# Second layer's weight conversion in five steps that pause while output tiles wait, its low bits from VectorE, and zero rows of q and k by DMA

## The chip, the cores and the metric

One core of one Trainium2 chip runs the whole program. The metric is the time of one execution on the device in microseconds (us), given as the median of several runs. The core's engines are TensorE (PE; its weight loads are listed as PEld), VectorE (DVE), ScalarE (ACT), GpSimd (POOL) and SyncE (SP). Each works through its own queue in order. SP and POOL issue the DMA transfers, which share 16 DMA engines.

## The reference

A gated linear attention over a sequence (768 steps, 4 batches, 8 heads of 48), then two feed-forward layers on its 3072 rows of 384 values, the second with a normalisation first:

```python
for t in range(S):
    state = alpha[:, :, t, :, None] * state + einsum('bhd,bhe->bhde', k[:, :, t], v[:, :, t])
    y[:, :, t] = einsum('bhd,bhde->bhe', q[:, :, t], state)
x = y.transpose(0, 2, 1, 3).reshape(B * S, H * D)
# layer 1
g = x @ w_gate; val = x @ w_val
x = (g / (1 + exp(-g))) * val @ w_out
# layer 2: the same after
xn = x / sqrt(mean(x * x) + 1e-6) * rms_g
```

The weights of the layers arrive as 64-bit floating-point numbers (`w1`, `w2` are handed over as pairs of 32-bit integers: a high word and a low word). The kernel has to make 32-bit numbers of them itself.

## The kernel before

**Blocks and pieces.** The 3072 rows are 24 chunks of 128 rows. Three chunks make a block of 384 rows, so each layer has eight blocks, named (0, 0) to (0, 7) for layer 1 and (1, 0) to (1, 7) for layer 2. A block runs over 12 slices f of the 1536 hidden values. For each slice `mlp_points` makes `g` (gate) and `v` (value) with 9 matmuls each (three terms of a high and low split of weights and inputs), and 9 matmuls of `o` (output) of the slice before. I call these 27 matmuls a period. ACT computes `s` from `g` (L593) and the rounded copy `hh` (L602); DVE multiplies `s` by `v` (L596) and makes the remainder `hl` (L608). There is one buffer of `g`, one of `v` and one set of three `o` tiles.

**The end of a block.** The three `o` tiles of a finished block wait in a list, `self.later`. `evac` takes one tile per point of the program: ACT copies it out to `ev` (L549; two buffers, each free again when its store has landed) and, in layer 1, squares it back into `o` (L552). Only then may TensorE write the next block's first piece into this tile, which happens at the end of the next block's second period.

**The conversion.** `conv(layer)` is a generator that turns the 12 raw weight slices into 32-bit ones: ACT takes the absolute value of the high word (L150, `room<-wraw`) and spreads the top three bits of the low word (L155, `wraw<-wraw`); DVE clamps (L156), shifts and joins the low bits (L158) and joins the sign (L163). For layer 2, whose input is split at once, ACT also makes the high part of the slice before (L178) and DVE its low part (L182). For layer 2 it goes through four steps for each slice, and `run` calls it three times per period with a rate (`CONV2` = 0.75 steps each time) during the blocks (0, 7) and (1, 0). The raw words come by SP's queue, three transfers a slice, two slices ahead. `norm_steps` (transposes `xt` on PE, `xhi` on ACT, `xlo` on DVE) prepares the inputs of layer 2 in the same blocks.

**What sets the order.** Every engine gets its instructions in the order in which this Python program emits them. A step of `conv` that is emitted between two uses of an engine stands between them in its queue.

**The start.** The tiles `qk` hold q, k and alpha of a chunk in 48 of each 64 partitions; the 16 others must be zero. POOL clears both whole tiles with memsets (L653, L654); the loads of `qk` (L93, SP's queue) follow these, since they write into the same tiles. POOL then issues the raw words of layer 1.

Of the kernel before, what the change touches and what calls it, by code (L numbers as in the profile page):

```python
# [13 lines left out]
AF = mybir.ActivationFunctionType  # L14
ALU = mybir.AluOpType
# [4 lines left out]
B, H, S, D = 4, 8, 768, 48  # L20
NT, DM, DFF = B * S, H * D, 1536
C = 128
NCB = S // C
NCH = B * NCB
NP = H // 2
# [10 lines left out]
PRE = 0.2  # L36
CONV1, CONV2 = 1.34, 0.75
EXTRA = 4
# [16 lines left out]
class Kernel:  # L55


    def __init__(self, tc, ctx, qka, vl, vlx, vn, qn, dirx, w1, w2, g2, mask, ident, out):
        self.tc, self.nc, self.ctx = tc, tc.nc, ctx
# [21 lines left out]
        self.ssq = const.tile([128, NCH], F32, name="ssq")  # L81
        self.mask_d, self.ident_d, self.g2_d = mask, ident, g2
        self.W, self.X, self.P = {}, {}, {}
# [49 lines left out]
    def conv(self, layer):  # L133
# [8 lines left out]
        nc = self.nc  # L142
        ahead = 2 if layer else 3
        R = {f: self.raw(layer, f) for f in range(ahead)}
        yield
        for f in range(NF):
            xf = self.xtile(layer, f)
            xi = xf.bitcast(I32)
            hi, lo = R[f][:, :, 1], R[f][:, :, 0]
            nc.scalar.activation(out=xf, in_=hi.bitcast(F32), func=AF.Abs, scale=65536.0)  # L150
            if layer and f:
                self.split_hi(layer, f - 1)
            yield
            top = R[f].rearrange("p f t -> p (f t)").bitcast(mybir.dt.uint8).rearrange("p (f b) -> p f b", b=8)[:, :, 3]
            nc.scalar.activation(out=lo, in_=top, func=AF.Copy, scale=1 / 32, bias=-15.5 / 32)  # L155
            nc.vector.tensor_scalar(out=xf, in0=xf, scalar1=W_MIN, scalar2=W_MAX, op0=ALU.max, op1=ALU.min)  # L156
            yield
            nc.vector.scalar_tensor_tensor(out=xi, in0=xi, scalar=3, in1=lo,  # L158
                                           op0=ALU.logical_shift_left, op1=ALU.bitwise_or)
            if layer and f:  # L160
                self.split_lo(layer, f - 1)
                yield
# [486 lines left out]
    def run(self):  # L649
        nc = self.nc  # L650
        nb = len(BLOCKS[0])
        self.where = {FIRST[0][j] + i: (j, i) for j, m in enumerate(BLOCKS[0]) for i in range(m)}
        nc.gpsimd.memset(self.qk[0], 0.0)  # L653
        nc.gpsimd.memset(self.qk[1], 0.0)  # L654
        nc.gpsimd.memset(self.pt32, 0.0)
# [39 lines left out]
        for gj, f, piece in self.mlp_points():  # L695
# [31 lines left out]
            if gj in ((0, 0), (0, 1)) and self.split_ok(gj, f):  # L727
                next(self.sp, None)
            if gj in ((0, nb - 1), (1, 0)) and self.ready[1] < self.freed + EXTRA - 1:
                conv(1, CONV2)  # L730
# [10 lines left out]
def _layout(inputs):  # L741
# [26 lines left out]
    for pre in ("moe_", "moe2_"):  # L768
# [8 lines left out]
    return dict(qka=qka, vl=vl, vlx=vlx, vn=vn, qn=qn, dirx=dirx, w1=ws[0], w2=ws[1], g2=g2, mask=mask,  # L777
                ident=np.eye(128, dtype=np.float32))

# [11 lines left out]
```

## Time and profile before

| | |
|---|---|
| time, median of 3 runs | 1154.93 us (1153.11 to 1155.69) |
| profiled execution | 1155.11 us; its span in the trace 1153.3 us |
| PE busy | 1096.6 us (95% of the span) |
| PEld busy | 1028.5 us (89%) |
| DVE busy | 635.0 us (55%) |
| ACT busy | 452.1 us (39%) |
| POOL busy | 47.3 us (4%) |
| chain that ended last | PE 83%, ACT 3%, DVE 2% |

Busy time is a sum over the whole program. The times of single instructions are given from the start of the span. A timeline row has start, duration, engine, line and operation; in square brackets stands how long the engine had been idle before it and which instruction ended that. The granted TensorE clock is a share of full speed: 1.00 and 0.50 are its two levels, 2.4 and 1.2 GHz. About a tenth of the program is the attention's start, some 120 us in which PE has gaps; from there to the end PE is nearly always busy, apart from the blocks (0, 7) and (1, 0), from 620 to 745 us.

### The profile page before, as it was taken

Reading aid. Unit: us, or ns where it says so; the run is one execution under the profiler, and the core shown is the slowest. Engines: PE = TensorE matmul, PEld = TensorE weight load, DVE = VectorE, ACT = ScalarE, POOL = GpSimd, SP = SyncE. Lnnn points to the kernel's source line nnn. Section 1 sums busy time; section 2 is a strip of 40 time slices with the busy share of each in tenths; the row PEclk is TensorE's granted clock in tenths of the full one; section 3 lists DMA queues with packets and bytes.
Section 4 is the critical chain, followed back from the end, with each engine's and each line's share of the span. In section 5 each row is a group of like instructions: output and inputs, shape, how many; then the busy total and the mean of one; then the engine's idle time right before and its main releaser. Section 6 shows DMA issues by size and latency. Waiting matters only on the chain.

```text
span 1153.3 us, 31352 instructions
## 1 busy us (share of the span) xinstructions
PE 1096.6 (95%) x13812; PEld 1028.5 (89%) x13812; DVE 635.0 (55%) x1336; ACT 452.1 (39%) x884; POOL 47.3 (4%) x79
## 2 busy tenths in 40 slices
PE   2579999999999999999999999999999999999998
PEld 2455569999999999999999989999999999999998
DVE  4779867876776767677663767622222223222221
ACT  3365625543343443433445555422222223222222
POOL 2112000000000000000000000000000000000000
PEclk9779999999999999999999998999999999999999
DMA  8767544444544443544423444010101010101000
GB/s 259 207 190 253 155 105 140 110 124 122 132 138 109 133 128 103 139 128 125 142 78 127 145 159 143 4 41 1 41 1 42 2 41 2 41 1 42 1 21 21
DMA packets 58936, 112.26 MB, mean 97 GB/s; under 512 B 7664, under 2 KB 47856, under 8 KB 58800
## 3 DMA queue, kind: packets, MB, share of 16 engines
q1 hardware_dynamic: 53616, 89.02, 27.0%
q0 software_dynamic: 5184, 21.24, 5.4%
q8 instruction: 108, 1.77, 0.7%
q14 instruction: 28, 0.23, 0.1%
HBM read 97.26 MB, written 12.98 MB: 96 GB/s over the span
## 4 chain that ended last, share of the span: by engine, by line
PE 83%; ACT 3%; DVE 2%; issue 1%; DMA 1%; ACTq 0%; DVEq 0%
PE g L587 25%; PE o L628 25%; PE v L587 24%; PE y L320 3%; PE sb L268 2%; PE y L309 1%; PE sa L268 1%; PE kv L333 1%; PE xt L537 1%; PE kp L432 1%; PE y L305 1%; DMA out<-ev 1%; ACT ev L549 0%; ACT room L150 0%; DVE s L596 0%
## 5 line engine op out<-in xcount | busy, mean ns | idle before, releaser
L596 DVE TENSOR_TENSOR s<-s,v 128x384 f32<-128x384 f32 x192 | 106.3, 554 | 390.8 <-PE v L587 363.5
L587 PE MATMUL g<-xhi,w 128*128 128x384 f32 x1080 | 308.6, 339 | 0.0
L587 PE MATMUL v<-xhi,w 128*128 128x384 f32 x1080 | 307.9, 339 | 0.3 <-DVE s L596 0.3
L628 PE MATMUL o<-w,hh 128*128 128x384 f32 x1080 | 280.8, 341 | 5.5 <-ACT o L552 4.7
L602 ACT ACTIVATE hh<-s 128x384 fp32r<-128x384 f32 x180 | 94.5, 525 | 295.0 <-DVE s L596 294.9
L628 PEld LDWEIGHTS o<-w,hh 128*128 128x128 f32 x1080 | 191.7, 188 | 10.7 <-ACT o L552 7.3
L587 PEld LDWEIGHTS g<-xhi,w 128*128 128x128 f32 x1080 | 199.0, 188 | 1.9
L587 PEld LDWEIGHTS v<-xhi,w 128*128 128x128 f32 x1080 | 198.6, 188 | 2.2 <-DVE s L596 0.5
L593 ACT ACTIVATE s<-g 128x384 f32<-128x384 f32 x192 | 94.0, 489 | 256.0 <-PE g L587 255.8
L587 PE MATMUL g<-xlo,w 128*128 128x384 f32 x540 | 181.7, 337 | 0.0
L628 PE MATMUL o<-w,hl 128*128 128x384 f32 x540 | 181.4, 336 | 0.3 <-DVE hl L608 0.3
L587 PE MATMUL v<-xlo,w 128*128 128x384 f32 x540 | 181.4, 336 | 0.0
L608 DVE TENSOR_TENSOR hl<-s,hh 128x384 fp32r<-128x384 f32 x180 | 99.9, 555 | 57.4 <-ACT hh L602 57.4
L628 PEld LDWEIGHTS o<-w,hl 128*128 128x128 f32 x540 | 101.5, 188 | 0.9 <-DVE hl L608 0.9
L587 PEld LDWEIGHTS g<-xlo,w 128*128 128x128 f32 x540 | 101.8, 189 | 0.3
L587 PEld LDWEIGHTS v<-xlo,w 128*128 128x128 f32 x540 | 101.7, 188 | 0.0
L220 DVE TENSOR_TENSOR qk<-qk,bpb 128x512 f32<-128x512 f32 x96 | 65.7, 685 | 6.0 <-ACT kc L243 3.7
L243 ACT ACTIVATE kc<-qk 128x512 f32<-128x512 f32 x72 | 45.5, 631 | 53.7 <-DVE qk L220 52.4
L320 PE MATMUL y<-pt,vl 128*32 128x64 f32 x2880 | 50.6, 222 | 5.0 <-issue 5.0
L320 PEld LDWEIGHTS y<-pt,vl 128*32 128x32 f32 x2880 | 45.7, 112 | 6.3 <-issue 6.3
L289 ACT ACTIVATE pt<-sb 32x128 f32<-32x128 f32 x96 | 25.8, 269 | 44.1 <-DVE pt L279 43.1
L220 DVE TENSOR_TENSOR qk<-qk,bpa 128x512 f32<-128x512 f32 x48 | 33.0, 687 | 4.9 <-ACT px L243 3.3
(100 smaller groups left out, 1030.1 us busy)
## 6 DMA issues: line engine op xcount, KB each, us to landing
vl<-vl SPq DMA_DIRECT2D x120, 192.0 KB, 4.4
qk<-qka SPq DMA_DIRECT2D x48, 288.0 KB, 4.9
room<-w POOLq DMA_DIRECT2D x36, 384.0 KB, 6.4
dir<-dirx SPq DMA_DIRECT2D x54, 192.0 KB, 3.2
wraw<-w SPq DMA_DIRECT2D x18, 384.0 KB, 3.8
room<-w SPq DMA_DIRECT2D x18, 384.0 KB, 3.9
vn<-vn SPq DMA_DIRECT2D x24, 192.0 KB, 3.9
x2d<-ev SPq DMA_DIRECT2D x24, 192.0 KB, 2.0
```

The costliest lines, as they stand in the source:

```text
L220: self.nc.vector.tensor_tensor(out=v, in0=v, in1=sub(t, o, [(1, 2), (2, nb), (0, b)]), op=ALU.mult)
L243: self.nc.scalar.activation(out=sub(t, 0, [(NP * 64, 2), (b, NP * 64 // b), (1, b)]), in_=v, func=AF.Copy)
L268: nc.tensor.matmul(out=sc[o:o + 32, p], lhsT=kc[d, p, gs], rhs=qc[d, p, gs if b < 64 else slice(0, 64)], start=True, stop=True, skip_group ...
L289: nc.scalar.activation(out=self.pt32[o:o + 32, :, g], in_=out[NL - 2][o:o + 32], func=AF.Copy)
L305: nc.tensor.matmul(out=Y[:, k], lhsT=yn[:, 128 * k:128 * k + 128], rhs=self.ident, is_transpose=True, start=(k == 0), stop=False, skip_gro ...
L320: self.nc.tensor.matmul(out=ov, lhsT=self.vlt[l][:, p, e], rhs=pt[:, p], start=False, stop=False, skip_group_check=True)
L587: nc.tensor.matmul(out=ps[:, :N], lhsT=a, rhs=x, start=(q == 0), stop=(q == len(ops) - 1))
L593: nc.scalar.activation(out=s[:, :N], in_=g[:, :N], func=AF.Silu)
L596: nc.vector.tensor_tensor(out=s[:, :N], in0=s[:, :N], in1=v[:, :N], op=ALU.mult)
L602: nc.scalar.activation(out=hh[:, :N], in_=s[:, :N], func=AF.Copy)
L608: nc.vector.tensor_tensor(out=hl[:, :N], in0=s[:, :N], in1=hh[:, :N], op=ALU.subtract)
L628: nc.tensor.matmul(out=O[gj][i], lhsT=a, rhs=x, start=(f == 0 and q == 0), stop=(f == NF - 1 and q == len(ops) - 1))
```

## The change

Four edits:

- The low bits of layer 2 no longer go over ACT. DVE gets an integer pass over the clamped word (shift left by 3, mask) and joins the low word, shifted right by 29, in the instruction that joined ACT's result before.
- Layer 2's conversion has a step more for each slice (five), and three steps a period are taken in place of 2.25.
- It takes no step while an `o` tile waits in `self.later`.
- The 16 zero rows of each half of `qk` come by four DMA transfers of 98 KB on POOL's queue, in place of the two memsets.

```diff
-CONV1, CONV2 = 1.34, 0.75
+CONV1, CONV2 = 1.34, 1.0
...
-            top = R[f].rearrange("p f t -> p (f t)").bitcast(mybir.dt.uint8).rearrange("p (f b) -> p f b", b=8)[:, :, 3]
-            nc.scalar.activation(out=lo, in_=top, func=AF.Copy, scale=1 / 32, bias=-15.5 / 32)
+            if layer == 0:
+                top = R[f].rearrange("p f t -> p (f t)").bitcast(mybir.dt.uint8).rearrange("p (f b) -> p f b", b=8)[:, :, 3]
+                nc.scalar.activation(out=lo, in_=top, func=AF.Copy, scale=1 / 32, bias=-15.5 / 32)
             nc.vector.tensor_scalar(out=xf, in0=xf, scalar1=W_MIN, scalar2=W_MAX, op0=ALU.max, op1=ALU.min)
+            if layer:
+                nc.vector.tensor_scalar(out=xi, in0=xi, scalar1=3, scalar2=0x7FFFFFF8,
+                                        op0=ALU.logical_shift_left, op1=ALU.bitwise_and)
             yield
-            nc.vector.scalar_tensor_tensor(out=xi, in0=xi, scalar=3, in1=lo,
-                                           op0=ALU.logical_shift_left, op1=ALU.bitwise_or)
+            if layer:
+                nc.vector.scalar_tensor_tensor(out=xi, in0=lo, scalar=29, in1=xi,
+                                               op0=ALU.logical_shift_right, op1=ALU.bitwise_or)
+            else:
+                nc.vector.scalar_tensor_tensor(out=xi, in0=xi, scalar=3, in1=lo,
+                                               op0=ALU.logical_shift_left, op1=ALU.bitwise_or)
             if layer and f:
+                yield
                 self.split_lo(layer, f - 1)
                 yield
...
-        nc.gpsimd.memset(self.qk[0], 0.0)
-        nc.gpsimd.memset(self.qk[1], 0.0)
+        for i in range(2):
+            for h in range(2):
+                nc.gpsimd.dma_start(out=self.qk[i][64 * h + D:64 * h + 64].rearrange("d i p c -> d (i p c)"), in_=self.zero_d)
...
-            if gj in ((0, nb - 1), (1, 0)) and self.ready[1] < self.freed + EXTRA - 1:
+            if gj in ((0, nb - 1), (1, 0)) and self.ready[1] < self.freed + EXTRA - 1 and not self.later:
                 conv(1, CONV2)
```

The changed file is ten lines longer, so its lines have other numbers: L593 is L602 there, L596 is L605, L602 is L611, L608 is L617, L549 and L552 are L558 and L561, L178 and L182 are L187 and L191, L156 is L157, L158 is L163, L163 is L172; L159 is the new integer pass.

ACT at the beginning of block (0, 7), before: `s` and `hh` are of its first two slices, `ev` and `o` the tiles of block (0, 6), `wraw` and `room` the conversion's.

```order
L602 ACTIVATE hh<-s 128x384
L150 ACTIVATE room_9437<-wraw 128x1152
L549 ACTIVATE ev<-o_8506 128x384
L552 ACTIVATE o_8506,ssq<-ev 128x384
L549 ACTIVATE ev<-o_8507 128x384
L552 ACTIVATE o_8507,ssq<-ev 128x384
L155 ACTIVATE wraw<-wraw 128x1152
L593 ACTIVATE s<-g 128x384
L549 ACTIVATE ev<-o_8508 128x384
L552 ACTIVATE o_8508,ssq<-ev 128x384
```

The same place with the change:

```order
L150 ACTIVATE room_9439<-wraw 128x1152
L611 ACTIVATE hh<-s 128x384
L558 ACTIVATE ev<-o_8508 128x384
L561 ACTIVATE o_8508,ssq<-ev 128x384
L558 ACTIVATE ev<-o_8509 128x384
L561 ACTIVATE o_8509,ssq<-ev 128x384
L602 ACTIVATE s<-g 128x384
L558 ACTIVATE ev<-o_8510 128x384
L561 ACTIVATE o_8510,ssq<-ev 128x384
```

The conversion's L150 has moved ahead of `hh`, and its L155 between the second and the third tile is gone.

ACT at the beginning of block (1, 0), before; the `o` tiles are those of block (0, 7):

```order
L602 ACTIVATE hh<-s 128x384
L150 ACTIVATE room_9438<-room 128x1152
L178 ACTIVATE w<-room_9437 128x1152
L549 ACTIVATE ev<-o_9524 128x384
L552 ACTIVATE o_9524,ssq<-ev 128x384
L549 ACTIVATE ev<-o_9525 128x384
L552 ACTIVATE o_9525,ssq<-ev 128x384
L155 ACTIVATE room<-room 128x1152
L593 ACTIVATE s<-g 128x384
L549 ACTIVATE ev<-o_9526 128x384
```

The same place with the change:

```order
L150 ACTIVATE room_9440<-room 128x1152
L187 ACTIVATE w<-room_9439 128x1152
L602 ACTIVATE s<-g 128x384
L611 ACTIVATE hh<-s 128x384
L558 ACTIVATE ev<-o_9526 128x384
L561 ACTIVATE o_9526,ssq<-ev 128x384
L558 ACTIVATE ev<-o_9527 128x384
L561 ACTIVATE o_9527,ssq<-ev 128x384
L602 ACTIVATE s<-g 128x384
L558 ACTIVATE ev<-o_9528 128x384
```

The two long passes stand ahead of the block's first `s` now, not between `hh` and the tiles, and nothing of the conversion is left between the tiles.

DVE at the same block's beginning, before; the second `s` row is that of its first slice:

```order
L156 TENSOR_SCALAR room_9437<-room_9437 128x1152
L596 TENSOR_TENSOR s<-s,v 128x384
L158 SCALAR_TENSOR_TENSOR room_9437<-room_9437,wraw 128x1152
L182 TENSOR_TENSOR w<-room_9438,w 128x1152
L608 TENSOR_TENSOR hl<-s,hh 128x384
L163 SCALAR_TENSOR_TENSOR room_9437<-wraw,room_9437 128x1152
L596 TENSOR_TENSOR s<-s,v 128x384
L608 TENSOR_TENSOR hl<-s,hh 128x384
```

With the change, from the pair of `room_9440` on, that slice's `s` is the first one:

```order
L157 TENSOR_SCALAR room_9440<-room_9440 128x1152
L159 TENSOR_SCALAR room_9440<-room_9440 128x1152
L605 TENSOR_TENSOR s<-s,v 128x384
L617 TENSOR_TENSOR hl<-s,hh 128x384
L163 SCALAR_TENSOR_TENSOR room_9440<-room,room_9440 128x1152
L605 TENSOR_TENSOR s<-s,v 128x384
L191 TENSOR_TENSOR w<-room_9439,w 128x1152
L617 TENSOR_TENSOR hl<-s,hh 128x384
```

Two conversion passes between two uses of `s` and `hl` have become one at most places, with the integer pass L159 as the added row. The order of PE and of SP is the same in both kernels.

## Rows read from the trace of the kernel before

**Rows 1.** Windows: length, busy us of PE, PEld, DVE, ACT, POOL; clock; DMA.

```profile
620.21:744.51 124.30, 119.06 (x668) 116.74 (x668) 86.13 (x115) 74.08 (x111) 0.00 (x0) 0.97 0.37 126
694.45:701.26 6.81, 6.81 (x29) 6.81 (x29) 3.36 (x5) 3.39 (x5) 0.00 (x0) 0.66 0.46 155
```

**Rows 2.** Timeline of PE: the first `g` of two neighbouring periods.

```profile
636.04 0.33 PE L587 MATMUL g<-xhi,w 128*128 128x384 f32 x1
...
640.72 0.33 PE L587 MATMUL g<-xhi,w 128*128 128x384 f32 x1
```

**Rows 3.** Waits of PE, 610 to 760 us: total us, times, longest.

```profile
PE o L628 <- ACT o L552: 4.3, 4, 1.7
```

**Rows 4.** Timeline of PE, beginning of blocks (0, 7) and (1, 0).

```profile
630.73 0.62 PE L628 MATMUL o<-w,hh 128*128 128x384 f32 x2 [1.52 <-ACT o L552]
...
683.26 0.33 PE L587 MATMUL v<-xhi,w 128*128 128x384 f32 x1
...
689.76 0.62 PE L628 MATMUL o<-w,hh 128*128 128x384 f32 x2 [0.85 <-ACT o L552]
...
693.33 1.01 PE L628 MATMUL o<-w,hh 128*128 128x384 f32 x2 [1.74 <-ACT o L552]
```

**Rows 5.** Groups by line, 620 to 745 us: count, busy us, mean ns, idle before.

```profile
L537 PE MATMUL xt<-ident,x2in 128*128 128x128 f32 x18 | 3.0, 273 | 0.3 <-DVE xlo L532 0.3
...
L608 DVE TENSOR_TENSOR hl<-s,hh 128x384 fp32r<-128x384 f32 x25 | 13.9, 556 | 9.0 <-ACT hh L602 9.0
...
L156 DVE TENSOR_SCALAR room<-room 128x1152 f32<-128x1152 f32 x12 | 9.1, 758 | 3.0 <-ACT room L150 2.9
```

**Rows 6.** Timeline of ACT, beginning of block (0, 7).

```profile
624.42 0.53 ACT L602 ACTIVATE hh<-s 128x384 fp32r<-128x384 f32 x1 [0.62 <-DVE s L596]
624.85 1.24 ACT L150 ACTIVATE room<-wraw 128x1152 f32<-128x1152 f32 x1
...
628.05 1.23 ACT L155 ACTIVATE wraw<-wraw 128x1152 int32<-128x1152 uint8 x1
...
629.56 0.47 ACT L549 ACTIVATE ev<-o 128x384 f32<-128x384 f32 x1
```

**Rows 7.** Timeline of ACT, beginning of block (1, 0).

```profile
686.39 1.25 ACT L150 ACTIVATE room<-room 128x1152 f32<-128x1152 f32 x1
687.54 1.15 ACT L178 ACTIVATE w<-room 128x1152 fp32r<-128x1152 f32 x1
```

**Rows 8.** Timeline of DVE, the same place.

```profile
681.09 1.36 DVE L158 SCALAR_TENSOR_TENSOR room<-room,wraw 128x1152 int32<-128x1152 int32 x1 [0.59 <-ACT wraw L155]
...
684.11 1.35 DVE L163 SCALAR_TENSOR_TENSOR room<-wraw,room 128x1152 int32<-128x1152 int32 x1
685.38 0.55 DVE L596 TENSOR_TENSOR s<-s,v 128x384 f32<-128x384 f32 x1
```

**Rows 9.** Timelines of POOL, SP and DVE at the program's start.

```profile
0.73 1.38 POOL L653 MEMSET qk<- 128x1536 f32 x1 [0.29 <-POOLq L783]
...
2.14 2.09 SPq L93 DMA_DIRECT2D qk<-qka  x4
...
7.26 0.69 DVE L229 TENSOR_TENSOR qk<-qk 128x512 f32<-128x512 f32 x1 [6.00 <-DMA qk<-qka]
...
22.37 0.56 DVE L375 TENSOR_TENSOR dir<-dir 128x384 f32<-128x384 f32 x1 [4.13 <-DMA dir<-qn]
```

**Rows 10.** Windows of the start, columns as in rows 1; the last is GB/s.

```profile
8.00:10.00 2.00, 0.66 (x32) 0.52 (x32) 1.08 (x3) 1.23 (x3) 0.01 (x1) 1.00 0.94 209
12.00:24.00 12.00, 3.99 (x160) 3.05 (x160) 5.70 (x15) 4.11 (x5) 0.54 (x1) 1.00 1.04 385
```

**Rows 11.** DMA issues of the page: KB each, median us from issue to landing.

```profile
room<-w POOLq DMA_DIRECT2D x36, 384.0 KB, 6.4
...
x2d<-ev SPq DMA_DIRECT2D x24, 192.0 KB, 2.0
```

More of the change, by code (lines that the diff above doesn't have):

```diff
@@ L55, with __init__ @@
 class Kernel:
-    def __init__(self, tc, ctx, qka, vl, vlx, vn, qn, dirx, w1, w2, g2, mask, ident, out):
+    def __init__(self, tc, ctx, qka, vl, vlx, vn, qn, dirx, w1, w2, g2, mask, ident, zero, out):
         self.tc, self.nc, self.ctx = tc, tc.nc, ctx
@@ L81, in __init__ @@
         self.ssq = const.tile([128, NCH], F32, name="ssq")
-        self.mask_d, self.ident_d, self.g2_d = mask, ident, g2
+        self.mask_d, self.ident_d, self.g2_d, self.zero_d = mask, ident, g2, zero
         self.W, self.X, self.P = {}, {}, {}
@@ L777, in _layout @@
     return dict(qka=qka, vl=vl, vlx=vlx, vn=vn, qn=qn, dirx=dirx, w1=ws[0], w2=ws[1], g2=g2, mask=mask,
-                ident=np.eye(128, dtype=np.float32))
+                ident=np.eye(128, dtype=np.float32), zero=np.zeros((64 - D, 3 * NP * C), np.float32))
 def kernel(**inputs):
```

## Prediction

> **What bounds the kernel now.** I read the busy shares first: PE is busy 95% of the span, so a change can gain only where PE stands still or runs slowly, or at the start. Second, the table of windows for the blocks that the change touches. From the first `g` of block (0, 7) to the first `g` of block (1, 1), that is 24 periods, 124.30 us pass [rows 1]; an undisturbed period takes 640.72 - 636.04 = 4.68 us [rows 2], 24 of them 112.32. So 11.98 us are lost in these two blocks. Third, where: PE's waits give 4.3 us to one cause, tiles `o` that ACT has not yet squared back and so freed (L552) [rows 3], and the timeline shows the long ones: 1.52 us at the beginning of (0, 7), and 0.85 and 1.74 us at that of (1, 0) [rows 4], with 0.2 us between these two. Behind these last three the granted clock falls to its lower level: the period from 694.45 to 701.26 takes 6.81 us at a mean clock of 0.66 [rows 1], 2.13 more than 4.68, and the `o` matmuls from 693.33 [rows 4] to 694.45 lose about 0.6 more, being 3 matmuls in 1.12 us where 4.68 / 27 = 0.173 each would make 0.52. The one wait of 1.52 us by itself was not followed by a fall. The rest of the 11.98: 18 transposes of `norm_steps`, 3.0 us busy [rows 5], of which neighbouring matmuls cover a part; short waits for DVE, 0.3 us each; and the fractions of a microsecond that PE takes to fill up after each wait.
>
> The transposes stay. Taking 2.2 us for them (between half and all of the 3.0), 11.98 - 2.2 = 9.8 us can be had here at most: 4.3 of tile waits, 2.7 of clock, 2.8 of restarts and short waits.
>
> **Why ACT is late with the tiles.** At (0, 7): L150 at 624.85 and L155 at 628.05 stand between `hh` and the third tile, whose `ev` comes at 629.56 [rows 6]; PE has stood idle for it since 630.73 - 1.52 = 629.21 [rows 4]. At (1, 0) it is a chain over two engines: DVE's L158 waited for ACT's L155 until 681.09, then L182, `hl` and L163 (684.11) came before `s` at 685.38 [rows 8], although its `v` was ready at 683.26 + 0.33 = 683.6 [rows 4]. So `hh` is late, and behind it ACT has L150 and L178, 1.15 us each from start to next start, before the first tile [rows 7], and L155 before the third.
>
> **The change part by part.**
>
> *L155 leaves ACT.* Twelve passes of 1.23 us [rows 6], 15 us of ACT's 74.08 in these blocks [rows 1]. ACT has room there, so the sum is worth nothing by itself; what counts is the two passes ahead of a tile.
>
> *Order and pause.* At (0, 7) the third `ev` came 629.56 - 624.42 = 5.14 us behind `hh` [rows 6], 2.3 of it L150 and L155 at 1.15 each [rows 7]; without them it is 2.85. L150 now stands ahead of `hh`: ACT was free from 624.42 - 0.62 = 623.8, so `hh` starts at 624.95, half a microsecond later, and the third `ev` at 627.8 in place of 629.56. Freed 1.17 us later (629.56 to 630.73), the tile is there at 629.0; PE wants it at 629.2. But `ev` has two buffers, so the third must wait for the first tile's store: written about 625.9, 2.0 us to landing and up to 0.3 to issue [rows 11], 627.9 to 628.2. The tile is free at 629.4 at worst: 0 to 0.2 us of the 1.52 stay. At (1, 0) no conversion pass stands between `v` and `s` or between `hh` and the tiles: `s` runs at 683.6, `hh` at 684.2, the third `ev` 2.85 later at 687.0, and its tile is free at 688.2. PE stood idle for the first tile from 689.76 - 0.85 = 688.9 [rows 4]. All three waits go, with 0.7 us to spare even for the last tile, and with them the fall of the clock, since no cluster of waits is left ahead of it. What is late next is DVE.
>
> *The integer pass on DVE.* Twelve instructions more. The trace shows no one-source integer instruction; its nearest row is the clamp on the same tile with the same shape and also two operations, 0.76 us [rows 5], against 1.35 for the two-source integer passes [rows 8]. Below nothing it can't be, it is added work. I take 0.76, the nearest in form. DVE then has 86.13 + 12 x 0.76 = 95.3 us of work in some 114.8 [rows 1], 83%. Locally it is tighter: a period with clamp, integer pass and two joins has 2 x 0.76 + 2 x 1.35 + 2 x 0.56 = 5.3 us against 4.68, 0.6 late, made up in the next, which has a step without DVE work. PE feels a late `s` only when it is later than one `o` and one `g`, 3.1 us. So I book 0.1 us. The join of the low bits keeps its form and price and no longer waits for ACT (0.59 us at its last wait there [rows 8]). The Trainium skill (VectorE: DVE Perf Modes, section The perf-mode tier table) gives one-source instructions from SBUF at 32 bits twice the rate of two-source ones; 0.76 against 1.35 agrees, for fp32. It says nothing apart of integer operations; by it the sum is as taken, by the two-source row it is rival A.
>
> *More steps a period.* 61 steps at 3 a period in place of 50 at 2.25: 20.3 periods against 22.2, plus two pauses of about one period. The conversion ends as early as before, so no slice of (1, 0) comes late. Raw loads keep their place in SP's order.
>
> *Zero rows by DMA.* SP's `qk` loads no longer wait for the memset that runs from 0.73 for 1.38 us: issue near 0.75 in place of 2.14 [rows 9], 1.39 earlier. New: the first `qk` multiply on DVE, and behind it the whole chain of DVE and ACT, waits for two zero transfers as well; and POOL's fifth to eighth raw-word transfers wait for the zeros' semaphores, booked at nothing, since the words of the second slice are wanted behind the first slice's conversion, which DVE's queue reaches only after `dir` at 22.37. The first multiply now starts at 7.26 and could start between 5.9 and 7.7 (0.73 + 0.55 + 6.4, the landing of a four times larger POOL transfer [rows 11]). Either way DVE then stands still for up to 4.13 us until `dir` lands at 22.37 [rows 9], so only `dir` counts. It lands at the end of a stretch with all DMA engines busy [rows 10]; 393 KB of zeros lengthen that by 1.0 us (at 385 GB/s) to 1.9 us (at 209), minus 1.39: -0.4 to +0.5, and I take +0.1. From there on a shift goes through to the end, as PE has no slack after 122 us.
>
> **Sum.** Profiled execution 1155.11 us, itself 0.18 above the median. In the two blocks -9.8 + 0.2 (third tile) + 0.1 (DVE) = -9.5; start +0.1: 1145.7; less 0.18 on the scale of the median: 1145.5 us.
>
> **Rivals.**
>
> *A. The integer pass runs at the two-source price, 1.35.* Then DVE has 86.1 + 16.2 = 102.3 us; a full period has 5.9 against 4.68. Twelve times 0.6 = 7.2 us more than booked, absorbed between wholly (19 us of idle time) and not at all; half, 3.6: 1149.1 us. For it: the operations are integer ones. Against: same tile, shape and source count as the clamp.
>
> *B. The tiles still wait.* The conversion ahead of them moves but fills ACT at the same place, so the 4.3 us of waits stay and the clock falls again: gain 9.8 - 4.3 - 2.7 = 2.8, 1152.2 us. Against it: the order, with its instructions counted out above.
>
> *C. Slower.* An integer instruction with two operations takes one pass for each, 2.7 us. DVE's work is 86.1 + 32.4 = 118.5, and 9.0 us in which `hl` waits for `hh` [rows 5] can't be filled: 127.5 us for 114.8. DVE becomes the bound, PE waits 12.7 us in place of 0.1, and the clock falls as before (2.7): 1145.5 + 12.6 + 2.7 = 1160.8 us. The point from which it turns: 86.1 + 12x + 9.0 = 124.3, x = 2.4 us. For it no row speaks.
>
> *D. The zero rows hold up the loads.* The stretch in which the `qk` loads land, 48 rows of 64 each, ran at 209 GB/s, the later one with loads over all 128 rows at 385 [rows 10]. If the rate goes down with the rows that a transfer reaches, 16 rows run at 209 x 16 / 48 = 70 GB/s: 5.6 us for 393 KB, less 1.39, so `dir` lands 4.2 us later: 1149.6 us. Against it: other queues' transfers can fill the DMA engines beside them. The Trainium skill (SBUF — State Buffer, section Door 1: The DMA port swizzle) has a rule that speaks against this edit: 16 neighbouring partitions reach 4 of 16 ports, about 109 GB/s. By this page an estimate is 3.6 us for the zeros and 1147.6 us in all; no row shows a transfer into 16 partitions.
>
> **How the numbers follow.** The forecast 0.60: down to 1143.0 (0.7 less if half of the transposes' time is covered, the start at -0.4, and 1.3 for half of the spread of the runs of before) and up to 1148.0 (0.8 more if all of their time stays, the start at +0.5, and the same spread). A 0.17, from 1145.5 to 1152.7 by what is absorbed; B 0.08; C 0.07; D 0.08. A range of 1143.0 to 1151.0 holds the forecast, most of A, and D. A difference of 0.2%, 2.3 us, is about what a measurement of this kernel can tell from none, so faster ends at 1152.6: faster 0.84 (the forecast, D, most of A, a little of B), same 0.09, slower 0.07.
>
> **What would show it.** Right: the 24 periods take 114.8 us; PE has no wait for L561 over 0.3 us and no window below clock 1.00 between 620 and 745; `s` of (1, 0)'s first slice starts within 0.2 us of its `v`; L159 has a mean of 0.76 us; DVE's first multiply starts before 7.3 and its `dir` multiply between 22.0 and 22.9. Wrong: L159 at 1.35 with `v` or `xt` waiting for DVE (A), waits for L561 (B), DVE idle only behind `hh` (C), or `dir` near 26 (D).

## The result, and the profile after

The changed kernel takes 1143.81 us (median of 4 runs, 1143.43 to 1145.21) beside 1154.89 (4 runs, 1153.11 to 1155.69): 11.1 us less, a ratio of 0.9908 with a 95% interval of 0.9891 to 0.9926. The forecast was 1145.5 with a range of 1143.0 to 1151.0.

The profiled execution took 1143.43 us (before 1155.11). In the spans, 1153.34 and 1141.67, the 11.67 us lie in three places, cut at three instructions that both kernels have:

| stretch | before | after | gain |
|---|---|---|---|
| start, up to the first `g` behind 118 us | 121.75 | 120.30 | 1.45 |
| from there to the first `g` of (0, 7) | 498.46 | 498.47 | 0.0 |
| the 24 periods of (0, 7) and (1, 0) | 124.30 | 115.09 | 9.21 |
| from the first `g` of (1, 1) to the end | 408.8 | 407.8 | 1.0 |

The last row belongs to the run and not to the change: in that execution of before PE waited 0.8 us behind 980 us for an output copy whose buffer's store had landed late. The code there is the same in both kernels, the trace of the changed kernel with memsets (kernel 2 below) has this wait again, and in the 13 traces of this document the stretch takes 407.7 to 408.9 us.

The window of the 24 periods (length; busy us of PE, PEld, DVE, ACT, POOL; clock; DMA share; GB/s) answers to [rows 1]:

```profile
618.77:733.86 115.09, 114.94 (x668) 114.27 (x667) 94.01 (x127) 61.44 (x99) 0.00 (x0) 1.00 0.40 135
```

PE is busy in 114.94 of 115.09 us at a clock of 1.00, where it was 0.97 before. The list of PE's waits between 600 and 760 us, which held the 4.3 us of [rows 3], is empty. ACT at the beginning of (1, 0), beside [rows 7] (start, duration, engine, line, operation; in brackets the idle time before and what ended it):

```profile
677.50 1.16 ACT L187 ACTIVATE w<-room 128x1152 fp32r<-128x1152 f32 x1
678.56 0.47 ACT L602 ACTIVATE s<-g 128x384 f32<-128x384 f32 x1
680.12 0.53 ACT L611 ACTIVATE hh<-s 128x384 fp32r<-128x384 f32 x1 [1.08 <-DVE s L605]
680.55 0.47 ACT L558 ACTIVATE ev<-o 128x384 f32<-128x384 f32 x1
...
681.58 0.47 ACT L558 ACTIVATE ev<-o 128x384 f32<-128x384 f32 x1
...
683.45 0.49 ACT L558 ACTIVATE ev<-o 128x384 f32<-128x384 f32 x1 [0.34 <-DMA x2d<-ev]
```

Nothing of the conversion stands between `hh` and the third `ev`, which comes 3.33 us behind `hh` (the working had 2.85 and the store's landing as a possible 0.3 more: here are these 0.34). DVE's `s` at that place waits for PE alone, and its group shows the price of the integer pass (line, operation, count | busy us, mean ns | idle time before them):

```profile
679.53 0.56 DVE L605 TENSOR_TENSOR s<-s,v 128x384 f32<-128x384 f32 x1 [0.34 <-PE v L596]
```

```profile
L617 DVE TENSOR_TENSOR hl<-s,hh 128x384 fp32r<-128x384 f32 x25 | 13.8, 553 | 5.7 <-ACT hh L611 5.7
...
L159 DVE TENSOR_SCALAR room<-room 128x1152 int32<-128x1152 int32 x12 | 9.1, 760 | 0.4
L157 DVE TENSOR_SCALAR room<-room 128x1152 f32<-128x1152 f32 x12 | 9.1, 756 | 2.3 <-ACT room L150 2.2
```

L159 costs 760 ns, as the clamp L157 does. The start is where the trace doesn't look as foretold (timelines of SP, POOL and DVE, beside [rows 9]; then the window beside [rows 10]):

```profile
0.74 1.80 SPq L93 DMA_DIRECT2D qk<-qka  x4
```

```profile
1.27 2.08 POOL L664 DMA_DIRECT2D qk<-zero  x4 [0.82 <-POOLq L793]
...
7.38 0.54 POOL L123 DMA_DIRECT2D room<-w  x1 [1.63 <-DMA qk<-zero]
9.75 0.54 POOL L123 DMA_DIRECT2D room<-w  x1 [1.84 <-DMA qk<-zero]
```

```profile
9.55 0.69 DVE L238 TENSOR_TENSOR qk<-qk 128x512 f32<-128x512 f32 x1 [8.28 <-DMA qk<-zero]
...
21.74 0.56 DVE L384 TENSOR_TENSOR dir<-dir 128x384 f32<-128x384 f32 x1 [1.15 <-DMA dir<-qn]
```

```profile
8.00:10.00 2.00, 0.00 (x0) 0.00 (x0) 0.45 (x1) 0.40 (x1) 0.25 (x1) 1.00 0.97 161
```

The loads are issued 1.4 us earlier, and still DVE's first multiply starts 2.3 us later, since it waits for the zeros. DVE then stands still for 1.15 us instead of 4.13, and the `dir` multiply starts 0.63 us earlier than before.

This lead is not the 1.45 us of the table. At the third `dir` multiply the changed kernel is 0.19 us behind (57.53 for 57.34), at the fourth 1.34 us ahead (72.14 for 73.48). Between the two PE stood still twice before the change, and once after it, for "issue", which is time in which it waited for nothing that the profile shows (timelines of PE, before, then after):

```profile
66.94 0.97 PE L320 MATMUL y<-pt,vl 128*32 128x64 f32 x51 [1.71 <-issue]
...
71.49 0.95 PE L268 MATMUL sa<-kc 64*32 64x32 f32 x51 [2.79 <-issue]
```

```profile
69.79 0.65 PE L277 MATMUL sa<-kc 64*32 64x32 f32 x52 [2.88 <-issue]
```

### The profile page after: what moved, and what is told of

It reads as the page before. It is cut to its first block, busy times and chain, and to the rows that moved or that the text cites. A ratio compares the mean times of both kernels' runs of the same rounds, so it can differ in the third digit from the quotient of the medians.

```text
span 1141.7 us, 31364 instructions
## 1 busy us (share of the span) xinstructions
PE 1091.4 (96%) x13812; PEld 1025.5 (90%) x13812; DVE 642.3 (56%) x1348; ACT 439.3 (38%) x872; POOL 46.5 (4%) x81
## 4 chain that ended last, share of the span: by engine, by line
PE 88%; ACT 1%; DVE 1%; issue 0%; DMA 0%; ACTq 0%; DVEq 0%
PE o L637 26%; PE g L596 26%; PE v L596 26%; PE y L329 3%; PE sb L277 2%; PE y L318 1%; PE sa L277 1%; PE xt L546 1%; PE kv L342 1%; PE y L314 1%; PE kp L441 1%; DVE x L166 0%; ACT ev L558 0%; DMA out<-ev 0%; ACT pt L298 0%
## 5 line engine op out<-in xcount | busy, mean ns | idle before, releaser
L605 DVE TENSOR_TENSOR s<-s,v 128x384 f32<-128x384 f32 x192 | 106.2, 553 | 380.8 <-PE v L596 360.1
L596 PE MATMUL g<-xhi,w 128*128 128x384 f32 x1080 | 307.6, 338 | 0.0
L596 PE MATMUL v<-xhi,w 128*128 128x384 f32 x1080 | 307.3, 338 | 0.0
L611 ACT ACTIVATE hh<-s 128x384 fp32r<-128x384 f32 x180 | 94.5, 525 | 294.0 <-DVE s L605 293.7
L596 PEld LDWEIGHTS g<-xhi,w 128*128 128x128 f32 x1080 | 198.1, 188 | 1.9
L596 PEld LDWEIGHTS v<-xhi,w 128*128 128x128 f32 x1080 | 197.9, 188 | 1.6
L602 ACT ACTIVATE s<-g 128x384 f32<-128x384 f32 x192 | 93.9, 489 | 255.7 <-PE g L596 255.6
L596 PE MATMUL g<-xlo,w 128*128 128x384 f32 x540 | 181.2, 336 | 0.0
L596 PE MATMUL v<-xlo,w 128*128 128x384 f32 x540 | 181.0, 335 | 0.0
L617 DVE TENSOR_TENSOR hl<-s,hh 128x384 fp32r<-128x384 f32 x180 | 99.7, 554 | 53.1 <-ACT hh L611 53.1
L596 PEld LDWEIGHTS g<-xlo,w 128*128 128x128 f32 x540 | 101.4, 188 | 0.3
L596 PEld LDWEIGHTS v<-xlo,w 128*128 128x128 f32 x540 | 101.4, 188 | 0.0
```

The source lines that it names most:

```text
L596: nc.tensor.matmul(out=ps[:, :N], lhsT=a, rhs=x, start=(q == 0), stop=(q == len(ops) - 1))
L602: nc.scalar.activation(out=s[:, :N], in_=g[:, :N], func=AF.Silu)
L605: nc.vector.tensor_tensor(out=s[:, :N], in0=s[:, :N], in1=v[:, :N], op=ALU.mult)
L611: nc.scalar.activation(out=hh[:, :N], in_=s[:, :N], func=AF.Copy)
L617: nc.vector.tensor_tensor(out=hl[:, :N], in0=s[:, :N], in1=hh[:, :N], op=ALU.subtract)
```

## The experiments

The theory: in the two blocks the order on ACT and DVE and the pause clear the tiles' way, and the clock follows; the start is set by `dir`. Each row below is one kernel. "Pair" is the 24 periods of (0, 7) and (1, 0), "dir" the start of DVE's first `dir` multiply, "marker" the first `g` behind 118 us, the three in the profiled execution. The medians of before beside them were 1154.3 to 1154.9 us.

| kernel | median us | ratio to before, 95% | pair | dir | marker |
|---|---|---|---|---|---|
| before | 1154.9 | 1 | 124.30 | 22.37 | 121.75 |
| changed | 1143.8 | 0.9891 to 0.9926 | 115.09 | 21.74 | 120.30 |
| 1 before, zeros by DMA alone | 1151.0 | 0.9960 to 0.9982 | 124.14 | 23.22 | 121.61 |
| 2 changed, memsets back | 1146.8 | 0.9914 to 0.9940 | 116.59 | 23.76 | 122.82 |
| 3 changed, no pause | 1151.6 | 0.9965 to 0.9988 | 124.26 | 23.65 | 122.01 |
| 4 changed, low bits on ACT | 1148.3 | 0.9928 to 0.9954 | 118.37 | 22.01 | 120.57 |
| 5 no pause, raw words held | 1146.3 | 0.9917 to 0.9951 | 117.93 | 23.53 | 122.71 |
| 6 second integer pass | 1151.0 | 0.9962 to 0.9985 | 121.39 | 22.18 | 120.16 |
| 7 before, low bits on DVE alone | 1150.8 | 0.9959 to 0.9980 | 120.42 | 24.47 | 123.14 |
| 8 before, pause alone | 1156.8 | 1.0002 to 1.0023 | 125.95 | 23.89 | 123.91 |
| 9 zeros in the first loads | 1147.3 | 0.9925 to 0.9950 | 115.18 | 24.72 | 122.78 |
| 10 as 9, raw words later | 1145.6 | 0.9903 to 0.9930 | 115.13 | 19.70 | 121.34 |
| 11 as 10, early table load | 1143.0 | 0.9885 to 0.9915 | 115.10 | 18.61 | 119.88 |

### The blocks

**3, the pause taken out.**

```diff
-            if gj in ((0, nb - 1), (1, 0)) and self.ready[1] < self.freed + EXTRA - 1 and not self.later:
+            if gj in ((0, nb - 1), (1, 0)) and self.ready[1] < self.freed + EXTRA - 1:
```

> The changed kernel without the pause. On ACT the passes L150 and L187 then stand between the second and the third o tile of block (0, 7), 2.3 us; at (0, 6) the order stays. Theory 1 (what stands ahead of a tile decides): one wait for L561 of 1.5 to 1.8 us returns, at the beginning of (1, 0), none at (0, 7); being alone it lets the clock stay at 1.00; 24 periods in about 117 us, time 1145.5 us. Rival (five steps and DVE's low bits are enough, the pause does nothing): no wait over 0.3 us, 1143.8 us.

Neither the theory nor the rival had this: in the profiled execution the pair is back at 124.26 us, all of its gain gone, and much more than ACT's passes explain. PE's only wait between 600 and 765 us (total, times, longest), then ACT and SP at (1, 0):

```profile
PE o L637 <- ACT o L561: 6.6, 1, 6.6
```

```profile
683.95 0.47 ACT L558 ACTIVATE ev<-o 128x384 f32<-128x384 f32 x1
...
684.97 1.23 ACT L150 ACTIVATE room<-wraw 128x1152 f32<-128x1152 f32 x1
686.11 1.16 ACT L187 ACTIVATE w<-room 128x1152 fp32r<-128x1152 f32 x1
687.17 0.47 ACT L602 ACTIVATE s<-g 128x384 f32<-128x384 f32 x1
692.52 0.49 ACT L558 ACTIVATE ev<-o 128x384 f32<-128x384 f32 x1 [4.88 <-DMA x2d<-ev]
```

```profile
683.80 1.47 SPq L123 DMA_DIRECT2D room<-w  x3
685.33 0.42 SPq L93 DMA_DIRECT2D x2d<-ev  x1
```

The two passes L150 and L187 do stand ahead of the third tile, but ACT is through with them at 687.6. The third `ev` then waits 4.88 us for its buffer, which the first tile's store has to free. This store is issued at 685.33, right behind three transfers of raw words of 384 KB each, and lands some 7 us later (median of such stores in this kernel: 1.9). The step of the conversion that the pause would have held back is the one that issues raw words. This execution is the longest of the six, 2.8 us above their median, and in it the three raw transfers themselves were slow: they landed 3.2, 5.9 and 7.1 us after their issue, where such transfers took 3.2, 3.8 and 4.5 in the changed kernel. So the 6.6 us are at the long end. A loss of its own follows: the period behind the wait takes 6.64 us at a mean clock of 0.68.

```profile
694.83:701.47 6.64, 6.64 (x28) 6.64 (x28) 3.07 (x4) 1.19 (x3) 0.00 (x0) 0.68 0.47 165
```

**5, no pause, but the raw words held.** This separates the two things that the pause does, since the passes on ACT stay between the tiles.

```diff
             if f + ahead < NF:
-                R[f + ahead] = self.raw(layer, f + ahead)
+                self.hold.append((R, layer, f + ahead))
+                self.fetch()
...
+    def fetch(self):
+        if self.hold and not (self.hold[0][1] and self.later):
+            r, layer, f = self.hold.pop(0)
+            r[f] = self.raw(layer, f)
...
+                self.fetch()
                 conv(1, CONV2)
```

> The changed kernel without its pause (as in the run without the pause), but with the raw weight words of layer 2 not issued while an o tile waits; the conversion's passes stay between the tiles. The run without the pause showed at (1, 0) one wait of 6.6 us for the third tile (693.5, so PE stood idle from 686.9), whose ev waited 4.88 us for the landing of the first tile's store, issued at 685.33 right behind three raw transfers of 384 KB issued at 683.80. Theory 1, the raw transfers ahead of the store make the wait: without them the third ev comes when ACT is free, ACT's second tile ends at 685.07, plus L150 and L187 (2.3) and s (0.4) is 687.8, its tile free 1.1 later at 688.9, so at most 2.0 us of wait; the pair of blocks takes 117 to 118 us (115.1 + 2.0 and a restart), 120 if the clock falls behind it; median 1146 to 1149. Rival, the passes of ACT between the tiles make the wait and the store is only last by chance: a wait near 6.6 us and 124 us for the pair stay, median 1151.6.

Theory 1 holds: 117.93 us and 1146.3. The waits of PE, then ACT's third tile of (1, 0), then SP there:

```profile
PE o L643 <- ACT o L567: 2.2, 2, 1.6
```

```profile
688.97 0.47 ACT L608 ACTIVATE s<-g 128x384 f32<-128x384 f32 x1
689.34 0.48 ACT L564 ACTIVATE ev<-o 128x384 f32<-128x384 f32 x1
```

```profile
685.22 0.33 SPq L93 DMA_DIRECT2D x2d<-ev  x1
...
690.26 1.62 SPq L123 DMA_DIRECT2D room<-w  x3
```

The store goes ahead of the raw words, and `ev` follows `s` without a wait. The second and third period of (1, 0) together take 18.7 us without the pause, 11.3 here and 9.5 in the changed kernel. So of the 9.2 us of the pair between the first and the last, 7.4 are the raw words ahead of the store, with the fall of the clock that follows, and 1.8 the passes on ACT. This kernel's pair is 2.8 us longer than the changed kernel's; the rest of that is one period at (0, 7), 1.3 us longer, where ACT waited 1.31 us for the first raw words to land. It belongs to the run, since the next kernel, which has the pause, shows the same. By the medians the shares are alike and smaller: the pause is worth 7.8 us (1151.6 to 1143.8), and 5.3 of these (1151.6 to 1146.3) come back when only the raw words are held.

**2, the memsets back in the changed kernel.**

```diff
-        for i in range(2):
-            for h in range(2):
-                nc.gpsimd.dma_start(out=self.qk[i][64 * h + D:64 * h + 64].rearrange("d i p c -> d (i p c)"), in_=self.zero_d)
+        nc.gpsimd.memset(self.qk[0], 0.0)
+        nc.gpsimd.memset(self.qk[1], 0.0)
```

> The changed kernel with the two memsets of before in place of the zero transfers. Theory 1: the blocks (0, 7) and (1, 0) keep their whole gain, 24 periods in 115.1 us and no fall of the clock; the start is that of before (first multiply near 7.3, dir near 22.4), so the time is 1145.2 us, 1.4 above the changed kernel. Rival (the start's gain was chance): 1143.8 us, as the changed kernel.

The median is 3.0 us above the changed kernel's. In the pair of the profiled execution (the longest of the five), 1.5 us longer, one place differs, at (0, 7), on ACT and on PE:

```profile
626.33 1.25 ACT L150 ACTIVATE room<-wraw 128x1152 f32<-128x1152 f32 x1 [1.44 <-DMA wraw<-w]
```

```profile
631.51 0.62 PE L637 MATMUL o<-w,hh 128*128 128x384 f32 x2 [0.61 <-ACT o L561]
```

The code of these blocks is the same in both kernels; the raw words, issued from 617.10 on, just landed later than ACT wanted them (the third transfer 8.2 us after its issue, 5.7 in the changed kernel), and L150 stands ahead of `hh` and the tiles. At this place the new order is still exposed.

**4, low bits on ACT again, pause and five steps kept.**

```diff
-            if layer == 0:
+            if True:
...
-            if layer:
-                nc.vector.tensor_scalar(out=xi, in0=xi, scalar1=3, scalar2=0x7FFFFFF8,
-                                        op0=ALU.logical_shift_left, op1=ALU.bitwise_and)
...
-            if layer:
-                nc.vector.scalar_tensor_tensor(out=xi, in0=lo, scalar=29, in1=xi,
-                                               op0=ALU.logical_shift_right, op1=ALU.bitwise_or)
-            else:
+            if True:
```

> The changed kernel with the low bits from ACT again (L155's pass there, the join of before on DVE, no integer pass), five steps and the pause kept. Theory 1 (the pass matters by its place, and by the tie that it makes between ACT and DVE): no long pass stands between the tiles, so no waits for them, but DVE's joins wait for ACT again and PE waits 1 to 3 us for s, hl or xt; 24 periods in 116 to 119 us, 1145 to 1147.5 us, no fall of the clock. Rival (order and pause are all): 115.1 us and 1143.8 us. Second rival (ACT's 15 us are what was gained): the tiles wait as before and the clock falls, 1150 us or more.

The pair takes 118.37 us, 3.3 more than with DVE's low bits, as the theory had it; the median, 1148.3, lies 0.8 above its range. No tile is waited for, and the clock stays at 1.00. PE waits elsewhere:

```profile
PE xt L540 <- DVE xlo L535: 1.5, 2, 1.3
PE g L590 <- ACT s L596: 0.5, 1, 0.5
PE o L631 <- DVE hl L611: 0.5, 1, 0.5
```

DVE's joins waited 5.5 us for the pass on ACT, where in the changed kernel they wait for nothing. So L155 on ACT costs these 3.3 us, not by standing ahead of tiles but as DVE's joins wait for it.

**7, the low bits alone, and 8, the pause alone, in the kernel before.** Their diffs are those of the change: in 7 the integer pass and the new join with `CONV2` = 0.75, four steps and no pause; in 8 only `and not self.later`.

> The kernel before with the low bits of layer 2 made on VectorE, and nothing else: four steps a slice at 0.75, no pause, memsets. Theory, order at ACT's tiles is what counts: L155 no longer stands ahead of the third tile in either block, so of the 1.52 us at (0, 7) some 0.4 stay and of the 1.74 at (1, 0) some 0.6, while the 0.85 and 0.2 us for the tiles behind L150 and L178 stay: 2.1 of 4.3 us. The pair takes 122.1 us if the clock still falls and 119.4 if not, in place of 124.3; median 1150 to 1152.7. Rival, the low bits' place on ACT is what made the whole loss: waits under 0.5 us, 115 to 116 us, 1146. Second rival, as in the run without the pause, another queue takes the tiles' place: 124 us, 1154.6.

> The kernel before with the pause alone: four steps a slice at 0.75 a piece, low bits on ScalarE, memsets. Theory, the pause needs the higher rate: the tiles come unobstructed (no wait for L552 over 0.3 us), but 50 steps at 2.25 a period take 22.2 periods and two pauses about one each, 24.2 for the 24 there are, so the last slices of layer 2 come late and PE waits for their low parts, once or twice, 2 to 6 us in all; the pair takes 118 to 122 us in place of 124.3, median 1149 to 1153. Rival, the pause is all of it and the steps are only another cut: 118.4 us as with low bits on ACT and five steps, 1148.3 plus up to 3 for the memsets.

7 gained 3.5 us; waits for tiles of 2.5 us in all stayed (0.83, 0.24 and 1.04 of them at (1, 0)), and behind these three the clock fell again, for less long than before. That is the theory's case between its two times:

```profile
PE o L636 <- ACT o L560: 2.5, 4, 1.0
```

```profile
693.00:698.74 5.74, 5.74 (x29) 5.74 (x29) 2.77 (x4) 2.95 (x4) 0.00 (x0) 0.81 0.47 158
```

8 gained nothing: 0.1% slower, no difference by the 0.2% that tells one here, with a pair 1.65 us longer than before. Tile waits of 0.8 us are left of the 4.3, so the pause does clear the tiles. But the theory named the place and set it too small: the last slices of layer 2 come late, and the period at 731.62 takes 10.73 us at a clock of 0.68.

```profile
PE g L587 <- DVE w L182: 4.3, 2, 3.2
...
PE o L628 <- ACT o L552: 0.8, 2, 0.6
```

```profile
731.62:742.35 10.73, 7.55 (x29) 7.23 (x29) 5.70 (x7) 3.04 (x4) 0.00 (x0) 0.68 0.01 2
```

With five steps at a higher rate and the low bits still on ACT (kernel 4) the same pause gives 118.37. So the parts don't add up: low bits alone 3.9 us of the pair, pause alone -1.65, pause with five steps 5.9, low bits with five steps and no pause 0.0 (kernel 3), all three 9.2.

**6, a second integer pass,** to price DVE's slack.

```diff
+                nc.vector.tensor_scalar(out=xi, in0=xi, scalar1=0, scalar2=0x7FFFFFF8,
+                                        op0=ALU.logical_shift_left, op1=ALU.bitwise_and)
```

> The changed kernel with a second integer pass over every slice (shift by 0 and the same mask), which leaves the result as it is: 12 more DVE instructions of 0.76 us, 9.1 us, in the two blocks. It prices DVE's slack, on which the term for the integer pass and rival A rest. Theory of the prediction: an excess of DVE work is absorbed about half; rival A put 7.2 us in at 3.6, so here 9.1 x 0.5 = 4.6 us: the pair takes 119.7 us in place of 115.1, median 1148.4. Rival, DVE's idle time absorbs all of it, as of the first pass: 115.1 to 115.6 us, 1143.8 to 1144.3. Second rival, DVE is the bound already: all of it shows, 124.2 us, 1152.9.

Of 9.1 us more DVE work 6.3 show in the pair (121.39 - 115.09) and 7.1 in the median. That lies between the theory's half and all of it. The largest part is a wait of PE for transposed inputs:

```profile
PE xt L548 <- DVE xlo L543: 3.6, 2, 1.8
PE o L639 <- ACT o L563: 0.6, 1, 0.6
PE o L639 <- DVE hl L619: 0.5, 1, 0.5
```

So the first pass went in nearly free and used up the slack; a second one costs two thirds of itself.

### The start

**1, the zeros by DMA alone, in the kernel before.** The diff is kernel 2's turned round.

> The kernel before with one edit: the zero rows of q and k come by the four DMA transfers, no memset. The blocks (0, 7) and (1, 0) should be as before: 24 periods in 124.3 us with the clock's fall. Theory 1 (the start's gain in the changed kernel is the transfers' earlier start): the dir multiply starts near 21.7 in place of 22.4, the first g of the second block comes about 1.4 us earlier, and the time is 1153.5 us, 0.12% under before. Rival (the 1.4 us were chance, from PE's gaps for instructions and the clock's steps at the start): dir moves by 0.6 us or less, the time lies between 1154 and 1156 us. Rival D of the prediction (zero rows hold up the loads): dir lands later than 22.4 and the time is above 1156.

The median is 3.6 us below before's, where 1.4 (0.12%) were expected; the profiled execution, at 1153.94 one of the two longest of 8 (1150.36 to 1154.2), shows no such gain, so the trace can't say where it lies. Its first multiply and its `dir` are both later than before's:

```profile
10.26 0.69 DVE L229 TENSOR_TENSOR qk<-qk 128x512 f32<-128x512 f32 x1 [8.99 <-DMA qk<-zero]
...
23.22 0.56 DVE L375 TENSOR_TENSOR dir<-dir 128x384 f32<-128x384 f32 x1 [1.92 <-DMA dir<-qn]
```

Over the traces of one kind the start moves by more than the edit: with the zeros by DMA (changed, 1, 3, 4, 5, 6) `dir` starts at 21.74 to 23.65, mean 22.72; with memsets (before, 2, 7, 8) at 22.37 to 24.47, mean 23.62. The markers' means are 121.23 and 122.91. So the edit is worth about 0.9 us at `dir` and 1.7 at the marker, from single traces that overlap.

**9 to 11, three further steps at the start,** each on top of the one ahead: the first two loads of `qk` bring the zeros with them (64 rows in place of 48, on SP) and POOL's zero transfers go; the raw words of layer 1's second and third slice move behind the `vl` loads on SP; ACT loads its table early.

```diff
-                nc.gpsimd.dma_start(out=self.qk[i][64 * h + D:64 * h + 64].rearrange("d i p c -> d (i p c)"), in_=self.zero_d)
+            if n < 2:
+                self.load(self.qk[n][64 * h:64 * h + 64], self.qkp_d[n, h])
...
-        R = {f: self.raw(layer, f) for f in range(ahead)}
+        R = self.R = {f: self.raw(layer, f) for f in range(ahead if layer else 1)}
...
+        for f in (1, 2):
+            self.R[f] = self.raw(0, f, True)
...
+        nc.scalar.activation(out=self.warm, in_=self.Sd[:, 0, 0, 0:1], func=AF.Copy)
```

> The changed kernel, its zero rows by another way: the first two loads of qk bring 64 rows for each half, zeros among them, on SP's queue, and POOL issues no zero transfers. Theory, the four POOL transfers gate the first multiply and dir gates the rest: the multiply starts at 5.9 to 7.0 us (before: 7.26 with an issue at 2.14; here the issue is at 0.74 and a third more bytes) in place of 9.55, DVE then stands still about 3 us longer ahead of dir, which lands at 21.7 to 23.5 as in the runs so far; the marker (first g behind 118 us) stays at 120.2 to 122.7 and the median at 1143 to 1145. Rival, the first multiply gates the start: all goes 3 us earlier, 1140.8.

> As e9_pad, and the raw words of layer 1's second and third slice (six transfers of 384 KB) move from POOL's queue at the start to SP's, behind the vl loads of the first chunk. Theory, dir's landing is a matter of the bytes that share the DMA engines with it: 2.36 MB at 385 GB/s are 6.1 us less ahead of it, so dir lands by 17.5 and DVE's own chain sets its multiply: 6.2 + (21.74 - 1.15 - 9.55 = 11.0) = 17.2 us in place of 21.74; the marker comes 4.5 us earlier, near 116, and the median is 1139.3; the second slice's words, wanted by ACT at 35.8, land by 30. Rival, other gates stand behind dir (PE's own gaps, the words of the second slice): the marker stays at 120 to 122, 1143.8.

> As e10_raw, and ACT does a one-column copy at the start, which takes its table load (1.28 us, ahead of the first copy of px at 10.90 in the changed kernel) off the chain. Theory: the first copy starts when the first multiply is done, so the chain up to dir loses the 1.0 us for which DVE waited there: dir's multiply at 16.2, marker near 115, median 1138.3. Rival, the chain behind dir isn't set by ACT: as e10_raw.

Both theories of 9 fall: without POOL's zeros the first multiply comes later still, and so does `dir`; the median is 3.5 us above the changed kernel's. POOL, first, and DVE in kernel 9:

```profile
1.29 4.37 POOL L126 DMA_DIRECT2D room<-w  x8 [0.24 <-issue]
```

```profile
10.45 0.69 DVE L241 TENSOR_TENSOR qk<-qk 128x512 f32<-128x512 f32 x1 [9.18 <-DMA qk<-qkp]
...
24.72 0.56 DVE L387 TENSOR_TENSOR dir<-dir 128x384 f32<-128x384 f32 x1 [3.29 <-DMA dir<-qn]
```

Eight of the nine raw transfers are now out by 5.7 us, where in the changed kernel POOL waited for the zeros between them. In kernel 10, with six of the nine moved back, the first multiply starts at 8.81, not at the expected 6.2, and `dir` at 19.70 without a wait for DMA, which is DVE's own chain (8.81 + the 11.0 of the expectation = 19.8). So `dir` depends on the raw words that share the DMA engines with it: that theory holds up to there. But 2.0 us less at `dir` than in the changed kernel give a marker 1.0 us later. PE shows where it goes, in kernel 10:

```profile
36.33 0.48 PE L280 MATMUL sa<-px 64*32 64x32 f32 x18 [4.71 <-issue]
```

In the changed kernel the same matmuls start at 35.16 behind 3.17 us of "issue". Up to there kernel 10 had kept its lead of 2.0 us; at the second `dir` multiply it is 1.1 us behind, at the third 0.3 ahead, and at the fourth, behind the gaps before 72 us, 1.0 behind. The rival of 10, other gates behind `dir`, holds.

What PE waits for in these gaps no experiment shows, but the traces point at its instructions. In all 13 traces PE has 70 gaps of "issue" of over 1 us that begin between 27 and 75 us, and 69 of them end 1.1 to 1.7 us behind the end of a packet of 16 KB in the DMA queue that the page lists as "instruction". In kernel 10 that packet runs from 33.91 to 35.09, in the changed kernel from 32.79 to 33.89, both times with the DMA engines full (share 1.04 and 0.97 from 24 to 36 us). That PE waits there for its instructions is argued from this and not shown.

In kernel 11 `dir` comes 1.1 us earlier than in kernel 10, as its theory had it, but at 18.61 and not at 16.2, and the marker at 119.88 and not near 115. It has the best median, 1143.0, but its interval (0.9885 to 0.9915) and the changed kernel's (0.9891 to 0.9926) overlap almost wholly: it isn't shown to be faster.

## Why the prediction was right, and where it wasn't

**The blocks: right.** 114.8 us for the 24 periods were foretold, 115.09 measured; a gain of 9.21 for 9.5. The tile waits, the fall of the clock and the short waits went as the terms said, L159 has the clamp's 0.76, and `s` of (1, 0) starts 0.1 us behind its `v` (679.09 + 0.33 = 679.42 to 679.53). Rivals A, B and C fall with these rows. The Trainium skill (VectorE: DVE Perf Modes, section The perf-mode tier table) has, for fp32 in SBUF, a one-source pass at twice the rate of a two-source one. Here the integer pass took 760 ns and the two-source integer joins 1350 [rows 8], 1.8 times as long.

**The step on order and pause: right in its sum, incomplete in its reason.** It counted ACT's passes ahead of a tile and took a store's landing as 2.0 us. That holds while the queue ahead of the store is empty. The pause keeps it empty: kernels 3 and 5 show 7.4 of the 9.2 us that the pause is worth in the profiled executions, and 5.3 of 7.8 by the medians, to be raw words ahead of a store. "Raw loads keep their place in SP's order" was true, yet nothing in the working said what another place would cost. Nor did the step on more steps a period say that the pause needs them: at the old rate the pause gains nothing (kernel 8).

**DVE: right, with a limit set too low.** 0.1 us was booked for 9.1 us of work, and at most a few tenths show, as PE's list of waits is empty. Rival A's "half" of an excess was too small: kernel 6 shows 6.3 of 9.1, so by this share A would have cost some 5 us, an estimate, where 3.6 was written.

**The start: wrong.** The forecast had the first multiply between 5.9 and 7.7 and a shift of +0.1 us (-0.4 to +0.5). The multiply started at 9.55, `dir` at 21.74 (22.0 to 22.9 were named as the sign of being right) and the marker came 1.45 us earlier. The landing of the zeros was taken from a larger POOL transfer, 6.4 us, from a quieter time; here it was a median of 8.2. The term booked at nothing, POOL's raw words waiting for the zeros' semaphores, had an effect at `dir`, and it was a gain: fewer bytes ran beside it. In the changed kernel three of the nine raw transfers land behind `dir`'s load (22.39 to 24.99 us for 21.71), in kernel 9 none does, and its `dir` comes 3.0 us later; three transfers of 393 KB at the 385 GB/s of [rows 10] make 3.1 us, an estimate. But "only `dir` counts", and "from there on a shift goes through", fail between `dir` and the marker: a lead of 2.0 us at `dir` was lost in kernel 10, and the 1.45 us of the changed kernel arose in PE's gaps between 57 and 72 us, not at `dir`. So that they are the edit's isn't shown; the markers' means speak for a gain of that size, from few traces. Behind the marker a shift does go through: up to the first `g` of (0, 7) all 13 traces take 498.4 to 498.6 us.

**Rival D.** The rate in the window from 8 to 10 us was 161 GB/s with the zeros in flight, for 209 before, so the rate did go down. But `dir` didn't come near 26; D's 4.2 us are not seen. No run has the zeros alone, so what the Trainium skill (SBUF — State Buffer, section Door 1: The DMA port swizzle) says of 16 neighbouring partitions is neither shown nor refuted.

**The sum.** On the profiled execution -9.4 was foretold; measured are -9.2 in the blocks, -1.45 at the start and -1.0 that belongs to before's own run. The median fell 1.7 us lower than forecast. Kernels 1 and 2 put the zeros at 3.0 to 3.6 us by medians where the traces show 0.9 to 1.7. In kernel 2's profiled execution 1.5 us more are the late raw words at (0, 7), but that execution lies 1.7 us above its median, so they needn't be in the 3.0. The rest is open.

## What to carry to other kernels

Of a step that may be moved or held back, count the transfers that it issues and not only its passes on the engines: a store that frees a buffer is worth as much as the queue ahead of it is empty. A pause in side work needs a higher rate elsewhere, or its end comes late. Where a start keeps the DMA engines full, which transfers are held back can matter more than when the first is issued; and a lead there is worth only what the gaps behind it leave of it.

## What the runs showed of the hardware that I had not expected

- A store of 192 KB landed 1.9 us after its issue in the median, and about 7 us after it behind three loads of 384 KB on the same queue, the last of which took 7.1 us itself (kernel 3).
- Four transfers of 96 KB into 16 partitions, from POOL's queue at the start, took a median of 8.2 us to land, nearly as long as loads of four times their size: those of `qk` with 64 rows in its place took 10.4 (kernel 9) and 8.9 (kernel 10), those with 48 rows over a whole program 4.9 to 5.1.
- The granted clock fell to its lower level behind one wait of 6.6 us (kernel 3) and behind waits of 0.83, 0.24 and 1.04 in one period (kernel 7), and it stayed at 1.00 behind one wait of 1.6 (kernel 5).
- At the start PE stood still for 1 to 5 us at a time without a wait that the profile shows, and 69 of 70 such gaps in 13 traces ended 1.1 to 1.7 us behind the end of a 16 KB packet of the queue "instruction".
